# Three float32 products on zeros in place of twelve float16 ones, and the score pairs of tiles 1 to 7 issued one step later

## The chip, the cores and the metric

The kernel runs on one core of a Trainium2 chip. The core has a matrix engine (TensorE, PE in the profile), a vector engine (VectorE, DVE), a scalar engine (ScalarE, ACT), GpSimd (POOL) and SyncE (SP), whose queue issues nearly all transfers. Each engine works through its own instructions in order; semaphores tie them together. The metric is the device time of one execution in microseconds, and smaller is better.

## The reference, cut to what is computed

Attention of 2 batches with 12 heads, 448 positions and 64 features per head, whose scores are mixed over the heads before the softmax and again after it. Two feed-forward layers (768 to 2048 to 768), one with ELU and one with SiLU, follow on the 896 tokens.

```python
scores = scale * np.matmul(q, k.transpose(0, 1, 3, 2))
scores = np.einsum('bhij,hg->bgij', scores, w_pre)
scores = scores - np.max(scores, axis=-1, keepdims=True)
attn = np.exp(scores)
attn = attn / (np.sum(attn, axis=-1, keepdims=True) + 1e-09)
attn = np.einsum('bhij,hg->bgij', attn, w_post)
return np.matmul(attn, v).astype(np.float32)
```

## The kernel before

The attention part works on 8 tiles T (2 batches, 4 tiles of up to 120 query rows each). A tile is cut into steps of 20 rows (a tile's last step may have 10): tiles 0 to 7 begin at steps 0, 6, 12, 18, 23, 29, 35 and 41, and there are 46 steps. The feed-forward layers come after it, on the same core; the change does not touch them.

For one tile the work runs like this. `qk_pair(T, p)` makes the scores of heads 2p and 2p+1 on PE (line 117) into two PSUM banks; `qk_evac` copies them to the SBUF tile `s`, one head on ACT (line 124) and one on DVE (line 126). Six pairs fill one tile's `s`. There are two homes for `s` (even and odd tiles), so the first pair of tile T+1 writes over what tile T-1 left, and its copies wait until the last transfer out of that home is done. `relayout(s)` (line 147) moves 20 rows of `s`, one transfer for each 10 rows, into one of three slots of `blk`, in the layout in which heads can be mixed. It is issued on SP's queue, two steps ahead of its use.

One step s then does, in this order on each engine: `premix(s)` on PE (line 160, reads `blk`); in some steps from step 8 on two `av_pair` (line 226); the step's score pair, if it has one; `postmix(s-1)` on PE (line 199); the row maxima `rmax(s)` on DVE (line 166); `exps(s)` on ACT (line 174); the copies of the score pair on ACT and DVE; the reciprocal on DVE (lines 182 and 183) and the scaled mixing weights `krn` on POOL (line 187), of which the last two come ahead of the copies in steps with `av_pair`; `post_evac(s-1)` on ACT and DVE (lines 99 and 101); `relayout(s+2)` on SP's queue; and then the loads that the step's table names. `relayout(s+2)` waits until `premix(s-1)` has read its slot. The first relayout of a tile also waits for the copies of that tile's last score pair.

Which step has which score pair is set by the counter `nqk` (line 288 and the lines that follow). It starts at -3, since the first three pairs of tile 1 are made ahead of step 0. So the pairs of tile 1 that are left stand in steps 0 to 2, those of tile 2 in steps 3 to 8, and so on, without a gap, up to the last pair of tile 7 in step 38.

At the start, while the first loads are under way, PE multiplies zeros (line 269): the tile `wz` is set to zero on DVE (line 251) and touched once by ACT (line 252); twelve products of 128x128 with 128x448 in float16 follow, and then the six score pairs of tile 0.

Of the kernel before, what the change touches and what calls it, by code (L numbers as in the profile page):

```python
# [7 lines left out]
F32 = mybir.dt.float32  # L8
F32R = mybir.dt.float32r
F16 = mybir.dt.float16  # L10
# [7 lines left out]
P = 128  # L18
B, H, S, D = 2, 12, 448, 64
# [9 lines left out]
HS = 64  # L29
BW = 5 * H  # L30
NBUF = 3
NWARM = 12
NE = 3
LEAD = 3
KO = (0, 2, 4, 1, 3, 5)
# [4 lines left out]
def attn_moe_moe(ctx: ExitStack, tc: tile.TileContext, q, k, v, w_pre, w_post, w1i, w1o, w2i, w2o, out):  # L40
# [4 lines left out]
    def pool(name, **kw):  # L45
        cm = tc.tile_pool(name=name, reuse_waits="tile", **kw)
        return cm, cm.__enter__()
# [9 lines left out]
    cm_s1, sp1 = pool("s1", bufs=1, side="right")  # L57
# [17 lines left out]
    def prows(t):  # L75

        return nblk(t) * BI
# [3 lines left out]
    def load_q(T, eng=None, parts=(slice(0, NP),)):  # L81
        b, t = tiles[T]
        qT[T] = wp.tile([P, NP, 2 * P], F32, name=f"qt{T}", tag="qT", bufs=3).rearrange("p a b -> p (a b)")[:, :NP * TI].rearrange("p (a b) -> p a b", a=NP)
        for p in parts:
            (eng or nc.sync).dma_start(qT[T][:, p], q[b, t, :, p])
# [20 lines left out]
    def qk_pair(T, p, where=("qk0", "qk1")):  # L106

        b, t = tiles[T]
        m = prows(t)
        if T not in smap:  # L110
            smap[T] = (sp0, sp1)[T % 2].tile([P, H, S], F32, name=f"s{T}", tag="s")
        pq = [ps.tile([P, S], F32, name=f"pq{T}_{p}_{e}", tag=w, bufs=1) for e, w in enumerate(where)]
        for c in range(2):
            n = HS if c == 0 else max(m - HS, 40)
            for e in range(2):
                half = slice(e * D, (e + 1) * D)
                nc.tensor.matmul(pq[e][HS * c:HS * c + n], qT[T][half, p, HS * c:HS * c + n], kT[b, p][half], start=True, stop=True, tile_position=(e * D, HS * c))  # L117
        sev.append((T, p, m, pq))
# [97 lines left out]
    def av_pair(T, p):  # L216

        b, t = tiles[T]
        m = rows(t)
        if p % 2 == 0:  # L220
            late = T + 1 == len(tiles)
            avt[T] = ps.tile([P, 2, TI], F32, name=f"av{T}_{p}", tag=("pre2", "av", "pre0")[p // 2] if late else "qk0" if T + 2 == len(tiles) and p == NP - 2 else "av", bufs=1)
        for j in range(4):
            for e in range(2):
                h = 2 * p + e
                nc.tensor.matmul(avt[T][e * D:(e + 1) * D, p % 2, :m], vall[b][:NV, h, j], amap[T][:NV, j * H + h, :m], start=j == 0, stop=j == 3, tile_position=(0, e * D))  # L226
        if p % 2 == 1:
            (xsp if T + 2 >= len(tiles) else xev).append((T, p - 1, m, avt.pop(T)))
# [18 lines left out]
        xsp.clear()  # L247


    wz = sp1.tile([P, S], F16, name="wz", tag="s")  # L250
    nc.vector.memset(wz, 0.0)
    nc.scalar.activation(wz[0:1, 0:1], wz[0:1, 0:1], AF.Copy)
    load_k(0, 0, nc.scalar)
# [10 lines left out]
    for c in range(2):  # L264
        for r in range(2):
            nc.vector.memset(pbank[c][HS * (1 - r):HS * (2 - r), (4 * r + 3) * BW:(4 * r + 4) * BW], 0.0)
    for n in range(NWARM):
        pw = ps.tile([P, 4 * CP], F32, name=f"warm{n}", tag=f"pre{n % 3}", bufs=1)
# [14 lines left out]
    QK_AT, X_AT, D_AT = {}, {}, {}  # L283

    def at(d, step, f):
        d.setdefault(int(step), []).append(f)

    nqk, nav = -LEAD, 0
    for T in range(NT_ - 1):
        b, t = tiles[T]  # L290
        f, l = first[T], last[T]
        for p in range(NP):
            if nqk >= 0:
                at(QK_AT, nqk, lambda T=T, p=p: qk_pair(T + 1, p))
            nqk += 1
        if T + 3 < NT_:
            at(D_AT, (3, 9, 13, 19, 24)[T], lambda T=T: load_q(T + 3))
        for p in range(NP):
            nav = 8 + 6 * T + p // 2 * 2 if T < 5 else NB + (-8, -6, -5, -4, -2, -1)[3 * T + p // 2 - 15]
            at(X_AT, nav, lambda T=T, p=p: av_pair(T, p))  # L300
# [775 lines left out]
```

## Time and profile before

| | |
|---|---|
| runs of the kernel before | 612.55, 617.24, 616.12 us, median 616.12 |
| the profiled execution's own time | 616.55 us |
| its span, from first to last instruction | 614.8 us |
| PE busy | 601.5 us, 98% |
| DVE, ACT, POOL busy | 425.5, 367.7, 63.4 us |
| attention steps | from about 15 us to 171 us of the span |

The span starts 1.75 us less than the time: that much lies around the instructions. Busy time of PE counts pipelined instructions and does not say that PE is never waited for; which engine sets the pace has to be read stage by stage. In the feed-forward part, from about 171 us on, PE is busy without a break.

### The profile page before, as it was taken

How to read it: one execution, taken by the hardware profiler on the slowest of the kernel's cores; microseconds unless marked ns; L12 is line 12 of the kernel's file. 1: busy time of each engine (PE TensorE's matmuls, PEld its weight loads, DVE VectorE, ACT ScalarE, POOL GpSimd, SP SyncE). 2: the span in 40 equal slices, each digit the busy share in tenths (PEclk: the TensorE clock that was granted, in tenths of full speed). 3: DMA queues.
4: the chain of work that ended last, by engine and by line, in shares of the span. 5: the costliest groups of instructions: out<-in, count | busy, mean ns of one | idle time of the engine just before them, and what ended most of it. 6: DMA issues, size and time to landing. Idle time of an engine off the chain costs nothing.

```text
span 614.8 us, 15117 instructions
## 1 busy us (share of the span) xinstructions
PE 601.5 (98%) x6222; PEld 514.8 (84%) x6222; DVE 425.5 (69%) x726; ACT 367.7 (60%) x686; POOL 63.4 (10%) x119
## 2 busy tenths in 40 slices
PE   7899999999999999999999999999999999999997
PEld 2456676676799899999999999999999999999996
DVE  4677677888847999886776674599888877424420
ACT  4577777788838966758774643476767664322300
POOL 1122222247460000000000000000000000000000
PEclk9899999999999999999999999999999999999999
DMA  6576656554503243432443334344334324444300
GB/s 240 189 211 204 201 173 208 185 186 152 184 3 113 92 155 103 144 105 71 127 125 123 95 90 150 104 130 154 127 103 149 94 93 141 153 149 153 116 30 31
DMA packets 37785, 82.33 MB, mean 134 GB/s; under 512 B 4132, under 2 KB 18388, under 8 KB 37716
## 3 DMA queue, kind: packets, MB, share of 16 engines
q1 hardware_dynamic: 36852, 80.50, 40.8%
q8 instruction: 49, 0.80, 0.5%
q10 hardware_dynamic: 864, 0.87, 0.5%
q14 instruction: 20, 0.16, 0.1%
HBM read 59.24 MB, written 2.75 MB: 101 GB/s over the span
## 4 chain that ended last, share of the span: by engine, by line
PE 83%; ACT 6%; DVE 6%; DMA 2%; issue 1%; SPq 0%; POOL 0%; ACTq 0%; DVEq 0%; POOLq 0%
PE po L504 37%; PE b L778 28%; ACT pe L174 4%; PE pq L117 3%; PE av L226 3%; PE pre L160 3%; PE post L199 3%; PE ph L490 3%; DVE nmx L166 2%; DMA blk<-s 2%; DVE a L101 2%; PE post L490 1%; PE warm L269 1%; DVE sum L182 1%; DVE s L126 1%
## 5 line engine op out<-in xcount | busy, mean ns | idle before, releaser
L778 PE MATMUL b<-x,we 128*128 128x448 f32 x360 | 93.7, 363 | 0.0
L504 PE MATMUL po<-x,we 128*128 128x448 f32 x288 | 81.0, 362 | 0.0
L174 ACT ACTIVATE pe<-pre,nmx 124x448 f32<-124x448 f32 (+1 forms) x92 | 57.5, 629 | 37.0 <-DVE nmx L166 36.4
L730 ACT ACTIVATE wr<-wr 128x768 f32<-128x768 f32 (+1 forms) x61 | 52.6, 865 | 40.8 <-DMA wr<-in_w2o_dram 25.7
L778 PEld LDWEIGHTS b<-x,we 128*128 128x128 f32 x360 | 67.5, 188 | 4.6
L778 PE MATMUL b<-rr,we 128*128 128x448 f32 x288 | 69.5, 362 | 0.0
L199 PEld LDWEIGHTS post<-krn,pe 60*64 60x64 f32 x2520 | 48.6, 136 | 19.9 <-issue 11.2
L461 DVE TENSOR_TENSOR we<-wc,we 128x640 fp32r<-128x640 f32 (+1 forms) x37 | 32.4, 875 | 47.0 <-ACT we L452 45.9
L504 PE MATMUL po<-ge,we 128*128 128x448 f32 x216 | 60.3, 362 | 0.0
L726 DVE SCALAR_TENSOR_TENSOR wc<-wr,wc 128x768 int32<-128x768 int32 (+1 forms) x62 | 56.2, 907 | 2.8
L504 PEld LDWEIGHTS po<-x,we 128*128 128x128 f32 x288 | 54.1, 188 | 3.6
L778 PEld LDWEIGHTS b<-rr,we 128*128 128x128 f32 x288 | 54.1, 188 | 3.5
L166 DVE TENSOR_REDUCE nmx<-pre 124x1 f32<-124x448 f32 (+1 forms) x92 | 52.6, 612 | 5.0 <-PE pre L160 4.8
L504 PE MATMUL po<-rr,we 128*128 128x448 f32 x216 | 55.9, 362 | 0.0
L504 PE MATMUL po<-gs,we 128*128 128x448 f32 x216 | 54.9, 362 | 0.0
L160 PE MATMUL pre<-blk,kpre 64*64 64x448 f32 (+1 forms) x360 | 46.9, 548 | 4.0 <-DMA blk<-s 3.3
L187 POOL TENSOR_SCALAR krn<-kps,sum 124x60 f32<-124x60 f32 (+1 forms) x92 | 38.4, 432 | 115.6 <-DVE sum L183 75.8
L117 PE MATMUL pq<-kt,qt 64*64 64x448 f32 (+2 forms) x384 | 48.1, 557 | 2.0 <-ACT s L124 2.0
L226 PEld LDWEIGHTS av<-a,v 128*64 128x64 f32 x768 | 36.9, 137 | 15.6 <-ACT pe L174 11.3
L199 PE MATMUL post<-krn,pe 60*64 60x60 f32 x2520 | 48.1, 220 | 0.8 <-issue 0.2
L504 PE MATMUL po<-ta,we 128*128 128x448 f32 x168 | 44.8, 362 | 0.0
L452 ACT CAST we<-wc 128x640 fp32r<-128x640 f32 (+1 forms) x37 | 28.3, 764 | 27.2 <-DVE wc L726 26.0
(129 smaller groups left out, 1024.2 us busy)
## 6 DMA issues: line engine op xcount, KB each, us to landing
blk<-s SPq DMA_DIRECT2D x90, 210.0 KB
wr<-in_w1i_dram SPq DMA_DIRECT2D x32, 384.0 KB
wr<-in_w2i_dram SPq DMA_DIRECT2D x32, 384.0 KB
wr<-in_w1o_dram SPq DMA_DIRECT2D x24, 384.0 KB
wr<-in_w2o_dram SPq DMA_DIRECT2D x24, 384.0 KB
wr<-in_w1o_dram SPq DMA_DIRECT2D x12, 256.0 KB
wr<-in_w2o_dram SPq DMA_DIRECT2D x12, 256.0 KB
qt<-in_q_dram SPq DMA_DIRECT2D x7, 360.0 KB
```

The lines of the kernel that those rows point to most:

```text
L117: nc.tensor.matmul(pq[e][HS * c:HS * c + n], qT[T][half, p, HS * c:HS * c + n], kT[b, p][half], start=True, stop=True, tile_position=(e * ...
L160: nc.tensor.matmul(pre[s][r][HS * c:HS * c + HS], kpre[o], blkb[o, s % NBUF, c], start=True, stop=True, tile_position=(HS * r, HS * c))
L166: nc.vector.tensor_reduce(nmx[s][:n, r:r + 1], pre[s][r][:n], axis=AX.X, op=ALU.max, negate=True)
L174: nc.scalar.activation(t[:n], pre[s][r][:n], AF.Exp, bias=nmx[s][:n, r:r + 1], scale=1.0, accum_out=sums[s][:n, r:r + 1])
L187: nc.gpsimd.tensor_scalar(t[:n], kps[:n], z[:n, r:r + 1], None, op0=ALU.mult)
L199: nc.tensor.matmul(w[c][HS * u:HS * u + HS, r, j * BW:(j + 1) * BW], pexp[s][r][o, m * HS:(m + 1) * HS], kr[s][r][o].rearrange("p h i -> p ...
L226: nc.tensor.matmul(avt[T][e * D:(e + 1) * D, p % 2, :m], vall[b][:NV, h, j], amap[T][:NV, j * H + h, :m], start=j == 0, stop=j == 3, tile_ ...
L461: nc.vector.tensor_tensor(lo[:, :m], wbits[n][:, :m].bitcast(F32), hi[:, :m], op=ALU.subtract)
L504: nc.tensor.matmul(po, wt[:, kk * P:(kk + 1) * P], g_op(moe, k0 + kk, hf, gi), start=(k0 == 0 and n_ == 0), stop=(k0 + kn == KF and n_ == ...
L726: nc.vector.scalar_tensor_tensor(cc, r[:, :, 1], 3, cc, op0=ALU.logical_shift_left, op1=ALU.bitwise_or)
L730: nc.scalar.activation(hf, hf, AF.Prelu, scale=2.0 ** -112, alpha=2.0 ** 32)
L778: nc.tensor.matmul(o, wt[:, u * KH + i * P:u * KH + (i + 1) * P], X[x, i][:, xi], start=start and n_ == 0, stop=n_ == 8, skip_group_check= ...
```

## The change

The constant `NWARM` goes from 12 to 3, the tile `wz` becomes float32, and the step of each score pair goes up by one. Nothing else is edited.

```diff
-NWARM = 12
+NWARM = 3
@@
-    wz = sp1.tile([P, S], F16, name="wz", tag="s")
+    wz = sp1.tile([P, S], F32, name="wz", tag="s")
     nc.vector.memset(wz, 0.0)
     nc.scalar.activation(wz[0:1, 0:1], wz[0:1, 0:1], AF.Copy)
@@
         for p in range(NP):
             if nqk >= 0:
-                at(QK_AT, nqk, lambda T=T, p=p: qk_pair(T + 1, p))
+                at(QK_AT, nqk + 1, lambda T=T, p=p: qk_pair(T + 1, p))
             nqk += 1
```

Step 0 now has no score pair, and step 39 has one. The next piece is from DVE, steps 20 and 21, where tile 4 (`s_1201`) is filled and tile 5 (`s_1625`) begins; `nmx` are the row maxima of the step, `pq_5_1` is the second head of pair 5. Before:

```order
L166 TENSOR_REDUCE nmx_1598<-pre_0_1541 124x1
L166 TENSOR_REDUCE nmx_1598<-pre_1_1542 124x1
L182 TENSOR_SCALAR sum_1601<-sum_1601 124x2
L183 RECIPROCAL sum_1601<-sum_1601 124x2
L126 TENSOR_SCALAR s_1201<-pq_5_1_1565 120x448
L101 COPY a_1533<-post_93 128x2x48x5
L166 TENSOR_REDUCE nmx_1660<-pre_0_1619 124x1
L166 TENSOR_REDUCE nmx_1660<-pre_1_1620 124x1
L126 TENSOR_SCALAR s_1625<-pq_0_1_1627 120x448
```

And in the changed kernel, where tile 4 is named `s_1254`:

```order
L166 TENSOR_REDUCE nmx_1572<-pre_0_1515 124x1
L166 TENSOR_REDUCE nmx_1572<-pre_1_1516 124x1
L182 TENSOR_SCALAR sum_1575<-sum_1575 124x2
L183 RECIPROCAL sum_1575<-sum_1575 124x2
L126 TENSOR_SCALAR s_1254<-pq_4_1_1539 120x448
L101 COPY a_1507<-post_93 128x2x48x5
L166 TENSOR_REDUCE nmx_1633<-pre_0_1593 124x1
L166 TENSOR_REDUCE nmx_1633<-pre_1_1594 124x1
L126 TENSOR_SCALAR s_1254<-pq_5_1_1600 120x448
```

The rows of a step are the same, but the copy of pair 5, for which the first relayout of tile 4 waits, now stands in step 21, behind the maxima of that step. The relayout itself has not moved: it is the last work of step 21 in both kernels.

The second place is on ACT at step 39 (`pe` are the exponentials, `a_2748` and `a_2722` the evacuation of the step before). Before, the step has no copy into `s`:

```order
L174 ACTIVATE pe_0_2945,sum_2944<-pre_0_2907,nmx_2941 124x448
L174 ACTIVATE pe_1_2947,sum_2944<-pre_1_2908,nmx_2941 124x448
L99 COPY a_2748<-post_92 128x2x48x5
L364 CAST x_2960<-xr_2447 128x240
L349 CAST x_5_2963<-xr_757 128x448
```

In the changed kernel the last copy of tile 7 stands between the exponentials and the evacuation:

```order
L174 ACTIVATE pe_0_2925,sum_2924<-pre_0_2881,nmx_2921 124x448
L174 ACTIVATE pe_1_2927,sum_2924<-pre_1_2882,nmx_2921 124x448
L124 ACTIVATE s_2517<-pq_5_0_2887 90x448
L99 COPY a_2722<-post_92 128x2x48x5
L364 CAST x_2942<-xr_2421 128x240
L349 CAST x_5_2945<-xr_731 128x448
```

Here a copy was added to the step, as one was on DVE and a pair of score products on PE.

## Rows read from the trace of the kernel before

**Rows 1.** Timeline, first 21 us: start, us, engine, line, operation, count, [idle before, releaser].
```profile
0.84 0.24 DVE L251 MEMSET wz<- 128x224 uint32 x1 [0.84 <-PEq L1062]
...
2.28 4.59 PE L269 MATMUL warm<-wz 128*128 128x448 f16 x12 [2.28 <-ACT wz L252]
...
7.22 0.14 PEld L117 LDWEIGHTS pq<-kt,qt 64*64 64x64 f32 x4 [0.23 <-issue]
...
13.35 1.59 SPq L147 DMA_DIRECT2D blk<-s  x2
...
16.15 0.14 PEld L160 LDWEIGHTS pre<-blk,kpre 64*64 64x64 f32 x2 [0.66 <-DMA blk<-s]
...
20.24 0.98 PE L160 MATMUL pre<-blk,kpre 64*64 64x448 f32 x2 [2.08 <-DMA blk<-s]
```

**Rows 2.** Chain that ended last, in order of time: start, us, what (attention part).
```profile
14.99 5.21 DMA blk<-s
...
64.02 5.43 DMA blk<-s
```

**Rows 3.** Stretches: from:to, length, busy (x instructions) by engine, PEclk, DMA share, GB/s.
```profile
20.50:23.50 3.00, 3.00 (x30) 1.27 (x29) 1.16 (x2) 0.84 (x3) 0.07 (x1) 0.50 0.53 198
...
58.00:68.00 10.00, 9.82 (x272) 6.46 (x268) 7.21 (x18) 7.19 (x20) 2.53 (x6) 1.00 0.74 236
...
85.00:87.00 2.00, 2.00 (x72) 1.30 (x72) 0.94 (x4) 2.00 (x7) 0.01 (x1) 1.00 0.00 0
```

**Rows 4.** Timeline around step 15: premix of steps 14, 16 and 18, and a copy.
```profile
61.96 0.97 PE L160 MATMUL pre<-blk,kpre 64*64 64x448 f32 x8
...
68.59 0.94 PE L160 MATMUL pre<-blk,kpre 64*64 64x448 f32 x8
...
69.77 0.62 DVE L126 TENSOR_SCALAR s<-pq 120x448 f32<-120x448 f32 x1 [1.34 <-PE pre L160]
...
75.88 0.94 PE L160 MATMUL pre<-blk,kpre 64*64 64x448 f32 x8
```

**Rows 5.** Timeline, tile 4 begins: copies of steps 20 and 21, first relayout, premix(23).
```profile
86.72 0.60 DVE L126 TENSOR_SCALAR s<-pq 120x448 f32<-120x448 f32 x1
...
87.38 1.68 SPq L147 DMA_DIRECT2D blk<-s  x2
...
89.76 0.54 ACT L124 ACTIVATE s<-pq 120x448 f32<-120x448 f32 x1
...
93.33 0.93 PE L160 MATMUL pre<-blk,kpre 64*64 64x448 f32 x8
```

**Rows 6.** Timeline, tile 5 begins: copy in step 27, premix(29), maxima of step 29.
```profile
109.61 0.54 ACT L124 ACTIVATE s<-pq 120x448 f32<-120x448 f32 x1
...
112.98 0.98 PE L160 MATMUL pre<-blk,kpre 64*64 64x448 f32 x8
...
114.20 0.61 DVE L166 TENSOR_REDUCE nmx<-pre 124x1 f32<-124x448 f32 x1
```

**Rows 7.** Timeline, tile 6 begins: copy in step 33, premix(35), maxima of step 35.
```profile
129.46 0.53 ACT L124 ACTIVATE s<-pq 90x448 f32<-90x448 f32 x1
...
132.88 0.98 PE L160 MATMUL pre<-blk,kpre 64*64 64x448 f32 x8
...
134.05 0.61 DVE L166 TENSOR_REDUCE nmx<-pre 124x1 f32<-124x448 f32 x1
```

**Rows 8.** Timeline, tile 7 begins: end of step 39's exponentials, premix(41), maxima of step 41.
```profile
149.61 0.20 ACT L174 ACTIVATION_READ_ACCUMULATOR pe<-pre,nmx 124x1 f32 x1
...
152.28 0.94 PE L160 MATMUL pre<-blk,kpre 64*64 64x448 f32 x8
...
153.88 0.61 DVE L166 TENSOR_REDUCE nmx<-pre 124x1 f32<-124x448 f32 x1
```

**Rows 9.** Timeline, tile 1 begins: copy in step 3, premix(6).
```profile
30.14 0.54 ACT L124 ACTIVATE s<-pq 120x448 f32<-120x448 f32 x1
...
35.36 0.93 PE L160 MATMUL pre<-blk,kpre 64*64 64x448 f32 x8
```

## The prediction

> **What bounds the kernel now.** I read the attention part stage by stage, since the feed-forward part, which the change doesn't touch, has PE busy without a break and simply starts later when attention ends later. First the timeline of the start: twelve products on zeros fill PE from 2.28 us for 4.59 us, the score pairs follow, and then PE waits for `blk`: the second half of premix(1) stood still for 2.08 us until a relayout landed at 20.24 [rows 1]. After that the timeline shows two kinds of stretch. Up to about 100 us PE sets the pace: premix(14) to premix(16), two steps, is 68.59 - 61.96 = 6.63 us, and PE has something to do in all of it. One pair of steps is longer, premix(16) to premix(18) with 7.29 us; there DVE stood still for 1.34 us ahead of the copy of tile 4's first score pair [rows 4], since that copy overwrites what tile 2's last relayout still reads. From 100 us to 156 us PE has small gaps, and the loop of maxima on DVE, exponentials on ACT and the reciprocal on DVE sets the pace; a late premix costs only what it is later than DVE is ready for it.
>
> The places that matter for the change are the tile changes. The first relayout of a tile waits for the copies of the tile's last score pair. For tile 4 it starts at 87.38 us, right behind the DVE copy of step 20 (86.72 + 0.60), and premix(23), which reads it, starts at 93.33: nearly six us of room [rows 5].
>
> **The change, part by part.** *The zeros.* Twelve products take 4.59 us, 0.38 each, or 448 columns at the lower of the two clock levels, 1.2 GHz. A float32 product goes through PE twice; at the full level one passage takes 0.14 + 0.23 = 0.37 us from weight load to weight load [rows 1], where 448 columns at 2.4 GHz would be 0.19. So a passage runs at half a column per cycle, a product at a quarter, and at 1.2 GHz it costs 4 x 0.37 = 1.5 us: three cost 4.5, the same as the twelve. The first float32 weight load has nothing ahead of it to hide under: between 0 and 0.2 us, I take **+0.1** (the weight load of 0.14 us is the nearest row [rows 1]). The memset of `wz` writes 448 words per row where it wrote 224: 0.24 us becomes some 0.5, ending near 1.3 us, and the products waited for ACT until 2.28 anyway [rows 1]; nothing, unless that wait were gone, and then 0.24.
>
> The Trainium skill, page "TensorE: Matmul & The Clock Gate", section "Back-to-back issue gap", gives a product's spacing at the lower level as its columns divided by 1.2 GHz and names no data type; by it three products would be over after 1.1 us. By the row of the passages they take 4.5. The trace decides for the passages here, and the other reading is priced below as a rival.
>
> *The step that gains and the step that loses a pair.* From step 1 to step 38 every step has one pair as before, with the same number of products and copies, so its work is unchanged. Step 0 loses one pair (on PE, ACT and DVE). That frees nothing: premix(1) waits for the relayout until 20.24 in any case [rows 1]. Step 39 gains one. PE has a gap there; ACT gets a copy of 0.53 us [rows 7] and DVE one of 0.60 [rows 5], both in the loop that sets the pace: **+0.55**.
>
> *The wait that goes.* Tile 4's first copy now comes in step 16, when tile 2's last relayout has long landed. The 7.29 us become 6.63 [rows 4]: **-0.66**. The other tile changes show no such wait, so nothing is to be had there.
>
> *The wait that comes.* For tiles 4 to 7 the last pair's copies now stand in the step that ends with the tile's first relayout, two steps ahead of its use. A relayout is two transfers issued about 0.84 us apart (1.68 for two [rows 5]). At the start, with an empty queue, one that was issued at 13.35 let PE go on at 16.15 [rows 1]: 2.80 us. So the second half is there 0.84 + 2.80 = 3.64 us after the issue, and the issue comes 0.06 us after the last copy (87.32 to 87.38 [rows 5]). That the queue is empty at these places shows in the stretch from 85 to 87 us, in which nothing moved [rows 3]. The copies of the step in question end where today's copies of that step end:
> - Tile 4: ACT's copy of step 21 ends at 89.76 + 0.54 = 90.30, issue 90.36, landed 94.00, premix(23) started at 93.33 [rows 5]. PE sets the pace: **+0.67**.
> - Tile 5: copy ends 110.15, issue 110.21, landed 113.85, premix(29) started at 112.98, so 0.87 late. Its 0.98 us ended 0.24 ahead of DVE's maxima at 114.20 [rows 6]: **+0.63**.
> - Tile 6: 129.99, 130.05, landed 133.69, 0.81 late against 132.88; 0.19 of room ahead of the maxima at 134.05 [rows 7]: **+0.62**.
> - Tile 7: step 39's exponentials leave ACT at 149.81, the new copy ends at 150.34, landed 154.04. Premix(41) stood at 152.28, and with the 0.55 of step 39 at 152.83: 1.21 late, 0.66 of room [rows 8]: **+0.55**.
>
> Tile 1 keeps its room: the copy of step 3 ends at 30.68, landed at 34.38, premix(6) at 35.36 [rows 9]. Tiles 2 and 3 likewise have a step more than tiles 4 to 7. Behind each late relayout the next ones stand on SP's queue, with loads of `v` or weights between them; each is issued 1.7 us or so after the one ahead and used two or three us after it, so they don't fall further behind. The `k` loads of steps 10 to 15 wait for PE's products of the same step instead of the step before; that holds SP up for about the length of one pair, with the relayouts behind them used more than a step later. I take nothing for it.
>
> What is uncertain is the landing. Lower end: no lateness counts, the sum is 0.1 + 0.55 - 0.66 = 0. Upper end: two relayouts are in the chain of waits with 5.21 and 5.43 us [rows 2], about 2.5 us more than 2.80. Four times 2.5 would add 10. Both of those had other transfers ahead of them (three relayouts' worth at the start, and without a break from 58 to 68 us, at a DMA share of 0.74 [rows 3]), while the tile changes 4 to 7 find the queue empty. I take 2.80.
>
> **The sum.** 0.1 + 0.55 - 0.66 + 0.67 + 0.63 + 0.62 + 0.55 = +2.46. The profiled execution took 616.55 us (the median of the runs is 616.12, so it is an ordinary one): **619.0 us**, 0.4% more.
>
> **The rivals.**
> - *Late landings, slower.* The relayouts at tile changes take some 5.3 us as the two in the chain did, not 2.80. For: DMA share at such times rises once the relayouts follow each other. Against: the empty queue. With two of four late it is 619.0 + 5.0 = 624.0, with all four 629. It decides (over 1% slower) from the second late one on. Chance 0.14.
> - *No lateness counts.* The landing is earlier than 2.8 us, or DVE and ACT have more room than I see: 616.6 us. For: in the stretch after 100 us PE has gaps. Against: tile 4 lies where PE has none. Chance 0.12.
> - *The zeros don't raise the clock.* Then the pairs start at half speed. The stretch from 20.50 to 23.50 shows what that is: granted clock 0.50 [rows 3], until PE had worked for some 3.5 us; half of it is lost, 1.7 us: 620.7 us. Against: that same stretch was float32 work, and the clock rose in it. Chance 0.05.
> - *The three products are over at once*, as three float16 ones would be: 3 x 0.38 = 1.15 us, so 3.4 us sooner. The first pairs begin up to 3.4 us earlier at the lower clock, do half as much, and gain at most 1.7: 617.2 us. It is what the page named above would make of them; the passages in the trace speak against it. Chance 0.04.
>
> **How the numbers follow.** The forecast, 616.6 to 622.7 with its middle at 619.0, has 0.65. The runs of the kernel before differ by 0.8%, so about 1%, 6 us, is what a measurement can tell from no change. Over 1% slower (above 622.3) are the late landings and a small tail of the forecast: 0.18. Over 1% faster (below 610) would need a gain that no row shows: 0.03. Within 1%: 0.79. The range that leaves out 2 in 10 goes from 615.0 (the case without lateness, less the scatter of the runs) to 624.0 (two late landings).
>
> **What would show it.** In the changed kernel's profile: three `warm` products, six records, ending near 6.9 us, and pairs with no wait behind them; no wait of DVE ahead of the first copy of tile 4; PE (premix, line 160) waiting for `blk` once at the beginning of each of tiles 4 to 7, by about 0.7 to 1.2 us; a copy into `s` on ACT in step 39. It is wrong if those waits are missing, if they are 2 us and more, if a wait for `blk` appears in the middle of a tile, or if the granted clock is 0.50 under the first pairs.

## The result, and the profile after

The changed kernel takes 621.54 us (median of 6 runs, 620.06 to 624.18) beside 615.35 us for the kernel before (6 runs, 612.55 to 617.24). The ratio is 1.0113, with a 95% interval from 1.0076 to 1.0151: some 7 us slower. The forecast was 619.0 with a range from 615.0 to 624.0. The direction and the range held; the size, +2.46 us, was less than half of what came.

| | before | after |
|---|---|---|
| the profiled execution's own time | 616.55 us | 624.18 us |
| its span | 614.8 us | 622.4 us |
| PE busy | 601.5 us | 606.9 us |
| DVE, ACT, POOL busy | 425.5, 367.7, 63.4 us | 427.4, 368.4, 63.6 us |
| maxima of the last attention step begin | 167.34 us | 174.76 us |

One of the executions profiled below, of the kernel before, lost some 12 us in the feed-forward part for reasons of its own, and only its attention part is read. In the changed kernel all of the loss lies in the attention part: from the last step's maxima to the end it is 447.4 us before and 447.6 after. The timeline of the start of the changed kernel answers to [rows 1]:

```profile
0.89 0.43 DVE L251 MEMSET wz<- 128x448 f32 x1 [0.89 <-PEq L1062]
...
2.27 4.85 PE L269 MATMUL warm<-wz 128*128 128x448 f32 x6 [2.27 <-ACT wz L252]
...
7.05 7.46 PE L117 MATMUL pq<-kt,qt 64*64 64x448 f32 x72
...
15.71 3.17 PE L160 MATMUL pre<-blk,kpre 64*64 64x448 f32 x14 [1.20 <-DMA blk<-s]
```

Three float32 products are six records and take 4.85 us where the twelve took 4.59. The pairs follow at once; the weight loads of their first rounds, and the stretch:

```profile
7.05 0.29 PEld L117 LDWEIGHTS pq<-kt,qt 64*64 64x64 f32 x8 [1.29 <-issue]
7.62 0.14 PEld L117 LDWEIGHTS pq<-kt,qt 64*64 64x64 f32 x4 [0.28 <-issue]
8.00 0.14 PEld L117 LDWEIGHTS pq<-kt,qt 64*64 64x64 f32 x4 [0.24 <-issue]
```
```profile
6.00:14.00 8.00, 8.00 (x74) 2.53 (x72) 4.84 (x8) 4.32 (x8) 0.00 (x0) 1.00 0.73 271
```

The columns are those of [rows 3]; the 1.00 is the granted clock. It also reads 1.00 over the zeros of the kernel before, whose pace, 0.38 us for 448 columns, is that of the lower level, so here the pace says more: the first round of the pairs takes 0.57 us and the later ones 0.38, as in [rows 1]. In the profile of the zeros alone the first two rounds take 0.80 and 0.49 us, so that some 0.5 us are lost there. The second half of premix(1) does not stand for 2 us this time. The waits of PE from 10 to 175 us (us in total, times, longest) show a kind that was not in the forecast:

```profile
PE post L199 <- issue: 3.8, 2, 2.0
PE pq L117 <- ACT s L124: 2.0, 5, 0.5
PE pre L160 <- DMA blk<-s: 1.7, 2, 1.2
...
PE av L226 <- issue: 0.6, 1, 0.6
```

"issue" is time in which PE waits for nothing that the profile shows. The timeline around the longest of these, with the first relayout of tile 4 behind it, and the stretch that follows:

```profile
85.72 0.86 PE L199 MATMUL post<-krn,pe 60*64 60x60 f32 x47
...
88.57 0.34 PE L199 MATMUL post<-krn,pe 60*64 60x60 f32 x9 [1.99 <-issue]
...
91.18 1.73 PE L199 MATMUL post<-krn,pe 60*64 60x60 f32 x56
...
92.58 1.66 SPq L147 DMA_DIRECT2D blk<-s  x2
```
```profile
89.20:92.60 3.40, 3.40 (x69) 2.15 (x65) 2.61 (x6) 2.19 (x6) 0.00 (x0) 0.52 0.02 5
```

PE stops after 47 of the 56 products of one postmix for 1.99 us; behind that the granted clock is 0.52, that is the lower level of 1.2 GHz nearly throughout, so that the next postmix takes 1.73 us where it takes 0.99 elsewhere. Tiles 5 and 7 look as forecast; first relayout, premix, and for tile 7 the maxima:

```profile
114.75 5.14 SPq L147 DMA_DIRECT2D blk<-s  x6
...
117.59 1.43 PE L160 MATMUL pre<-blk,kpre 64*64 64x448 f32 x6 [0.18 <-ACT xr L237]
...
156.20 5.18 SPq L147 DMA_DIRECT2D blk<-s  x6
...
159.06 1.81 PE L160 MATMUL pre<-blk,kpre 64*64 64x448 f32 x8 [0.51 <-DMA blk<-s]
...
160.90 1.16 DVE L166 TENSOR_REDUCE nmx<-pre 124x1 f32<-124x448 f32 x2 [0.98 <-PE pre L160]
```

The premix begins 2.84 and 2.86 us after the issue, and its second half lies 0.83 us further on.

For the rest one table serves. It gives the time between the starts of the maxima of two steps, from the timeline of each profile (steps 8 to 14 hold tile 2's change, 14 to 18 tile 3's, 22 to 25 tile 4's, 28 to 34 tile 5's, 34 to 40 tile 6's, 40 to 43 tile 7's). "After 2" is a second profile of the changed kernel, and the other columns are experiments below.

| steps | before | after | after 2 | zeros alone | pairs alone | tiles 4-7 | tiles 5-7 | tile 7 | pairs, v later | pairs, pad |
|---|---|---|---|---|---|---|---|---|---|---|
| 8-14 | 19.67 | 23.03 | 20.38 | 20.14 | 21.22 | 19.67 | 19.93 | 19.98 | 20.73 | 20.64 |
| 14-18 | 14.39 | 13.50 | 14.21 | 13.17 | 13.53 | 13.46 | 13.17 | 13.17 | 14.27 | 13.49 |
| 18-22 | 13.12 | 16.13 | 13.18 | 13.17 | 14.42 | 13.12 | 13.18 | 13.18 | 13.18 | 13.53 |
| 22-25 | 10.26 | 11.99 | 13.12 | 10.14 | 13.36 | 12.98 | 10.32 | 10.13 | 12.75 | 13.12 |
| 28-34 | 19.85 | 20.52 | 20.37 | 19.85 | 20.35 | 23.58 | 20.37 | 19.88 | 21.26 | 21.95 |
| 34-40 | 20.25 | 20.94 | 22.39 | 20.25 | 21.85 | 20.94 | 20.97 | 20.49 | 21.75 | 20.93 |
| 40-43 | 10.05 | 11.52 | 11.51 | 10.04 | 11.50 | 11.54 | 11.56 | 11.58 | 11.52 | 13.43 |

### The profile page after: what moved, and what is told of

Its sections match the earlier page's. It is cut to its first block, busy times and chain, and to the rows that moved or that the text cites. A ratio compares the mean times of both kernels' runs of the same rounds, so it can differ in the third digit from the quotient of the medians.

```text
span 622.4 us, 15096 instructions
## 1 busy us (share of the span) xinstructions
PE 606.9 (98%) x6216; PEld 515.8 (83%) x6216; DVE 427.4 (69%) x726; ACT 368.4 (59%) x686; POOL 63.6 (10%) x119
## 4 chain that ended last, share of the span: by engine, by line
PE 87%; ACT 5%; DVE 4%; issue 2%; DMA 2%; ACTq 0%; DVEq 0%
PE po L504 37%; PE b L778 27%; PE av L226 5%; PE pre L160 4%; PE post L199 4%; PE pq L117 4%; PE ph L490 3%; ACT pe L174 3%; DMA blk<-s 2%; DVE nmx L166 1%; PE post L490 1%; DVE a L101 1%; PE warm L269 1%; DVE sum L182 0%; DVE s L126 0%
## 5 line engine op out<-in xcount | busy, mean ns | idle before, releaser
L160 PE MATMUL pre<-blk,kpre 64*64 64x448 f32 (+1 forms) x360 | 50.4, 546 | 2.0 <-DMA blk<-s 1.7
```

Of the source, the lines that this page charges most:

```text
L160: nc.tensor.matmul(pre[s][r][HS * c:HS * c + HS], kpre[o], blkb[o, s % NBUF, c], start=True, stop=True, tile_position=(HS * r, HS * c))
```

## The experiments

### The two parts apart, and second profiles

Both kernels unchanged once more, and then each part of the change alone. The zeros alone:

```diff
-NWARM = 12
+NWARM = 3
-    wz = sp1.tile([P, S], F16, name="wz", tag="s")
+    wz = sp1.tile([P, S], F32, name="wz", tag="s")
```

and the pairs alone:

```diff
-                at(QK_AT, nqk, lambda T=T, p=p: qk_pair(T + 1, p))
+                at(QK_AT, nqk + 1, lambda T=T, p=p: qk_pair(T + 1, p))
```

> The kernel before once more, for a second profile of it. In the first one the second half of premix(1) stood until a relayout landed at 20.24 us and the granted clock fell to 0.50 behind it. If that belongs to the kernel, it comes again, within some tenths of a us. If it is a matter of chance, PE doesn't wait there this time and the span up to the maxima of step 7 is about 2.5 us shorter, as it was in the changed kernel. Time ratio to itself 1.000.

Ratio to itself 0.9998 (0.9975 to 1.0021). Its profile answers the question: the maxima of step 1 begin 2.31 us after those of step 0 (17.36, 19.67), as in the zeros alone (17.91, 20.23) and in tile 7 alone (16.45, 18.77), but 4.84 us after them in the first profile (17.16, 22.00). So the 2.08 us of [rows 1] are no fixed part of the kernel. A wait like it stands in three of the fourteen profiles; the other two are 4.56 us with the pairs of tiles 1 to 3 moved and 3.84 us with `v` later.

> The changed kernel once more, for a second profile of it. In the first one PE stood still three times in the middle of the products of one step, with nothing in the profile to wait for: 0.58 us at 40.8, 1.77 at 46.7 and 1.99 at 86.6 us, each time after the same number of instructions beyond a multiple of 256. Theory A (chance: the code of PE comes in blocks by DMA, and a block was held up by other transfers): such stalls come at other multiples of 256, or not at all, and without them the time is about 3 us above the kernel before. Theory B (they belong to the new order): they come again at 40 to 47 and at 86 us. In both, the first relayouts of tiles 5, 6 and 7 are late by 0.6 to 1.2 us. Time ratio 1.011.

Ratio 1.0115 (1.0082 to 1.0148). None of the three stalls came again, and it was as slow all the same. What came again are the tile changes, and tiles 4 and 6 are far above the forecast (22-25 and 34-40). So the kernel is slower without these stalls too, and the 3 us that theory A left for that case are too few. In the first profile after, where they cost most, the wait at tile 4 is smaller (11.99 us).

> The zeros alone: three float32 products for twelve float16 ones, the score pairs in the steps of before. By the forecast +0.1 us; by the trace of the changed kernel, in which the pairs began at 7.05 us in place of 6.79, up to +0.4. Ratio 1.000 to 1.001. The rival (the three products change where PE's code blocks begin, by twelve instructions, and with it the stalls) would show stalls of PE without a cause in the profile and some us more.

Ratio 1.0000 (0.9978 to 1.0021): the zeros cost nothing that these runs can tell from zero, which is to within some 1.3 us.

> The pairs alone: the score pairs one step later, twelve float16 products on zeros as before. If the pairs cost what the forecast said, +2.4 us, ratio 1.004. If they cost all that was measured, +6 us, ratio 1.010. In its profile: no wait ahead of tile 4's first copy, and first relayouts that are late by 0.6 to 1.2 us at tiles 5, 6 and 7.

Ratio 1.0108 (1.0076 to 1.0139), 6.6 us of 614.2: the pairs are the whole loss.

### Which tiles

The zeros are those of before in all that follow. With the condition shown the pairs of tiles 1 to 3 move; with `T >= 3`, `T >= 4` and `T >= 6` in its place those of tiles 4 to 7, of tiles 5 to 7 and of tile 7.

```diff
-                at(QK_AT, nqk, lambda T=T, p=p: qk_pair(T + 1, p))
+                at(QK_AT, nqk + (T < 3), lambda T=T, p=p: qk_pair(T + 1, p))
```

> The pairs of tiles 1 to 3 alone one step later; those of tiles 4 to 7, and the zeros, as before. Theory A (the time is lost where tiles 4 to 7 begin, because their first relayout is late): nothing or little, 0 to +0.6 us, ratio 1.000 to 1.001; the first relayouts of these three tiles have a step more to spare. Theory B (any pair that is moved costs, for instance because SP's queue stands behind it in steps 10 to 15): three sevenths of the +6.6 us of all pairs, +2.8, ratio 1.0045.

Ratio 1.0088 (1.0057 to 1.0119), more than either theory had. The edit brings something of its own: tile 3's last pair moves to step 15, where tile 4's first pair stays, so that two pairs share two PSUM banks in one step and PE waits for the copies of the first. The longest wait of PE between 10 and 175 us, and DVE's copy of tile 4's first pair:

```profile
PE pq L117 <- ACT s L124: 3.5, 5, 1.9
```
```profile
72.28 0.62 DVE L126 TENSOR_SCALAR s<-pq 120x448 f32<-120x448 f32 x1 [3.52 <-DMA blk<-s]
```

The copy waits for tile 2's last relayout, as in [rows 4]. Steps 14 to 18 take 16.67 us there in place of 13.17, and the profiled execution also has the late relayout at the start. In the other stretches it is 20.45 (8-14), and 13.12, 10.28, 19.86, 20.25 and 10.05, as before. By its time this run decides nothing. Where the profiles show a cost of tiles 1 to 3 is steps 8 to 14: the eight profiles that leave these pairs where they were have 19.67 to 20.34 us there, the five others 20.38 to 21.22, not counting the first profile after with two of its stalls. Half a us or so is lost there, and no run tells why.

> The pairs of tiles 4 to 7 alone one step later; those of tiles 1 to 3, and the zeros, as before. Theory A: the whole loss, +6 to +6.6 us, ratio 1.010; in the profile the first maxima of tiles 4 to 7 later by about 2.5, 0.7, 1.4 to 2.1 and 1.6 us. Theory B: four sevenths, +3.8 us, ratio 1.006.

Ratio 1.0121 (1.0076 to 1.0166): tiles 4 to 7 alone cost as much as all pairs. Here the change only leaves step 15 without a pair. Theory A holds as to the place. In the profile tile 5's first relayout is late by 1.9 us (its second half is used 5.59 us after the issue), PE waits for it twice, and behind that the granted clock is 0.50 for 3.4 us:

```profile
116.80:120.20 3.40, 3.40 (x68) 2.14 (x63) 2.16 (x4) 1.77 (x5) 0.00 (x0) 0.50 0.77 248
```

Steps 28 to 34 take 23.58 us there, 3.2 more than the 20.37 of a landing on time: with the lower clock behind it, a late landing can cost well over its own delay.

> The pairs of tiles 5 to 7 alone one step later; those of tiles 1 to 4, and the zeros, as before. Theory A: tile 4's 2.9 us stay away, tiles 5, 6 and 7 cost 0.7, 0.7 and 1.6 us, and 1.5 to 2 us more for each of the three whose first relayout has a block of PE's code in its midst: +3 to +5 us, ratio 1.005 to 1.008. In the profile the maxima of step 24 come as in the kernel before. If the loss doesn't hang on the tile changes one by one: ratio 1.010 and more.

Ratio 1.0081 (1.0053 to 1.0109), at the upper edge of the expectation. The profiled execution (616.33 us) was among the lowest of twelve, up to 622.22. In it steps 22 to 25 take 10.32 us, so tile 4's loss is gone, and tiles 5, 6 and 7 cost 0.5, 0.7 and 1.5 us.

> The pairs of tiles 5 to 7 one step later, once more, for a second profile: the executions so far lie between 616.0 and 622.2 us, and the one that was profiled is among the lowest (616.33). Theory E (a block of PE's code that is fetched in the midst of a first relayout makes it late, by chance of when and where it is fetched): where this execution takes 620 us and more, at least one of the first relayouts of tiles 5, 6 and 7 has its second half used 4.5 to 5.6 us after the issue in place of 3.7, with a block ahead of it. Rival: the relayouts are as in the first profile and the time is lost elsewhere (the first relayouts of all, at 16 to 22 us, or PE at the end of a block).

Ratio 1.0050 (1.0027 to 1.0073), and the profile (616.84 us) is as the first to a few hundredths from step 14 on, with no late relayout. So about 3 us is the price of the three tiles without one: 3.1 by this run, 2.7 by the sum of the stretches. What the slower executions of the run before lost, 620 to 622 us, no profile caught; theory E was not tested by this run.

> The pairs of tile 7 alone one step later. By the profiles so far 1.6 us (1.1 where the first relayout is used, 0.55 in the step behind it), 2 us more in executions where a block of code hits that relayout: ratio 1.003 to 1.005. The forecast had 0.55 for the relayout and 0.55 for the copy in step 39, ratio 1.002.

Ratio 1.0028 (1.0012 to 1.0043), 1.7 us. Its timeline: first relayout, premix(41) and maxima, premix(42) and maxima.

```profile
145.96 5.17 SPq L147 DMA_DIRECT2D blk<-s  x6
...
148.85 1.82 PE L160 MATMUL pre<-blk,kpre 64*64 64x448 f32 x8 [0.54 <-DMA blk<-s]
150.71 1.16 DVE L166 TENSOR_REDUCE nmx<-pre 124x1 f32<-124x448 f32 x2 [1.03 <-PE pre L160]
...
153.26 0.94 PE L160 MATMUL pre<-blk,kpre 64*64 64x448 f32 x8
154.27 1.16 DVE L166 TENSOR_REDUCE nmx<-pre 124x1 f32<-124x448 f32 x2
```

The maxima begin 4.75 us after the issue. From the maxima of step 40 (146.46) it is 4.25 us where it was 3.12 before (150.76 to 153.88), and on to the next 3.56 where it was 3.01: behind the late premix PE still has the av products and the postmix ahead of premix(42). The same kernel, whose pairs of tile 4 stand where they stood, also answers to [rows 4]; premix of steps 14, 16 and 18:

```profile
58.28 0.93 PE L160 MATMUL pre<-blk,kpre 64*64 64x448 f32 x8
...
64.86 0.93 PE L160 MATMUL pre<-blk,kpre 64*64 64x448 f32 x8
...
71.45 0.93 PE L160 MATMUL pre<-blk,kpre 64*64 64x448 f32 x8
```

6.58 and 6.59 us, with the copy of tile 4's first pair in step 15 as before. So the 7.29 us of [rows 4] are not a fixed part of the kernel. They are no single case either: of the eight profiles that keep this copy in step 15, five take 13.17 us for steps 14 to 18, the first one 14.39, the one of tiles 1 to 3 16.67, and that of the kernel before with a pad (below) 14.20, where the same copy waits again:

```profile
69.27 0.62 DVE L127 TENSOR_SCALAR s<-pq 120x448 f32<-120x448 f32 x1 [1.57 <-DMA blk<-s]
```

The trace has the times at which the parts of a transfer report that they are done, ten reports for each transfer of a relayout. For the first transfer of tile 2's last relayout the last report comes 5.2 to 5.7 us after its issue in these three, and 3.9 to 4.3 in the five.

### Tile 4 and the loads of v

In the profile of tiles 4 to 7 tile 4 begins like this; relayouts and loads of `v` on SP's queue, and the premixes of steps 23 and 24:

```profile
88.16 1.68 SPq L147 DMA_DIRECT2D blk<-s  x2
...
89.89 0.54 SPq L95 DMA_DIRECT2D v<-in_v_dram  x1
...
90.51 1.65 SPq L147 DMA_DIRECT2D blk<-s  x2
...
91.14 1.57 PE L160 MATMUL pre<-blk,kpre 64*64 64x448 f32 x6
...
96.31 0.97 PE L160 MATMUL pre<-blk,kpre 64*64 64x448 f32 x4 [1.09 <-DMA blk<-s]
```

The first premix comes 2.98 us after the first issue, as it should. The one behind it is late: its second half starts at 96.31, 5.80 us after its relayout was issued behind a load of `v`. So I moved the loads, in the kernel with the pairs alone:

```diff
-                    at(D_AT, 2 * g + u + (16 if b else 0), lambda b=b, u=u, g=g: load_v(b, u, g))
+                    at(D_AT, 2 * g + u + ((16 if 2 * g + u < 5 else 21) if b else 0), lambda b=b, u=u, g=g: load_v(b, u, g))
```

> All pairs one step later, and the three loads of v that stand on SP's queue behind the first relayouts of tile 4 (steps 21 to 23) moved to steps 26 to 28, well ahead of their use in step 32. Theory D (tile 4 costs 2.9 us where tile 5 costs 0.7, because the relayout of its second step is issued behind a load of v and shares the DMA engines with it: its second half starts 5.3 to 5.9 us after its issue): now 3.7 us after its issue, tile 4 costs 0.7 to 1.2 us, and the time is some 2 us below that of the pairs alone, ratio 1.007 to 1.008. If v has nothing to do with it: step 24 as late as before, ratio 1.011.

Ratio 1.0128 (1.0099 to 1.0157): no gain. The same place in its profile:

```profile
89.39 7.41 SPq L147 DMA_DIRECT2D blk<-s  x8
...
92.95 0.97 PE L160 MATMUL pre<-blk,kpre 64*64 64x448 f32 x4 [0.37 <-DMA blk<-s]
...
94.99 0.59 PE L160 MATMUL pre<-blk,kpre 64*64 64x448 f32 x2 [1.07 <-DMA blk<-s]
...
97.36 0.92 PE L160 MATMUL pre<-blk,kpre 64*64 64x448 f32 x5
```

Step 24 no longer waits for its relayout, but that is no support for theory D: in this execution the first relayout was late instead (its second half came 5.60 us after the issue), and one wait hides the other: 22-25 is 12.75 us. The last report of the second relayout comes 5.55 us after its issue here too.

The edit also moved the loads behind another tile's first relayouts: tile 5's are issued in steps 27 and 28. First relayout, load of `v`, second relayout, and the second half of premix(30):

```profile
111.73 1.70 SPq L147 DMA_DIRECT2D blk<-s  x2
...
113.48 0.53 SPq L95 DMA_DIRECT2D v<-in_v_dram  x1
114.11 1.65 SPq L147 DMA_DIRECT2D blk<-s  x2
...
118.97 0.97 PE L160 MATMUL pre<-blk,kpre 64*64 64x448 f32 x4 [0.24 <-DMA blk<-s]
```

PE goes on there 4.86 us after the issue, and steps 28 to 34 take 21.26 us in place of 20.35 to 20.52. The ten reports of the transfer come 4.17 to 4.82 us after the issue of the relayout where they come after 3.5 to 3.6 without a load of `v`. So the load ahead does make a relayout later, by 0.7 to 1.2 us. At tile 4 in the profile above nine of the ten come by 4.71 us and the last at 5.75, so that its last us has another cause. What moving the loads clear of all first relayouts is worth was not shown.

### Blocks of PE's code

The profile has a queue named "instruction", with 49 packets of 16 KB that move 0.80 MB; PE has 12,432 products and weight loads, 254 for each packet, and the packets come faster where PE issues more of them. I take them for blocks of PE's code. In the second profile of the changed kernel the first relayout of tile 4 and its premix look like this, and between 91.2 and 91.3 us the DMA view has one such packet:

```profile
88.44 1.65 SPq L147 DMA_DIRECT2D blk<-s  x2
...
91.98 0.97 PE L160 MATMUL pre<-blk,kpre 64*64 64x448 f32 x4 [0.33 <-DMA blk<-s]
...
94.04 0.59 PE L160 MATMUL pre<-blk,kpre 64*64 64x448 f32 x2 [1.09 <-DMA blk<-s]
```
```profile
q1 hardware_dynamic: 13, 0.02, 56.1%
q8 instruction: 1, 0.02, 54.9%
```

The halves come 3.54 and 5.60 us after the issue. To see whether the code does it, I put 160 instructions more into PE's stream ahead of the first premix, in the pairs alone and in the kernel before:

```diff
+NPAD = 40
@@
+    pad = [ps.tile([P, 4 * CP], F32, name=f"pad{r}", tag=w, bufs=1) for r, w in enumerate(("av", "pre2"))]
+    for n in range(NPAD):
+        r, c = n % 2, n // 2 % 2
+        nc.tensor.matmul(pad[r][HS * c:HS * c + HS, :BW], kpre[HS * r:HS * r + HS], kpre[HS * r:HS * r + HS, :BW], start=True, stop=True, tile_position=(HS * r, HS * c))
```

> All pairs one step later, and ahead of the first premix, in a time in which PE waits, 40 small products (160 instructions of PE) on kpre whose result nobody reads: all later code of PE stands 160 instructions further on in its blocks of 256, so that its blocks are fetched some 3 us earlier in relation to the tiles. Theory C (the first relayouts of tiles 4 and 6 were later than those of tiles 5 and 7 because a block of PE's code was fetched in the midst of them): at tiles 4 and 6 the second half now starts 3.7 us after the issue, as at tiles 5 and 7 (it was 5.6 and 5.15), no block of code comes in the midst, and the time is 2 to 3 us below that of the pairs alone, ratio 1.006 to 1.008, unless PE stands at other block ends. If the landing depends on the tiles and not on the code: tiles 4 and 6 as before, ratio 1.011.

Ratio 1.017 (1.0121 to 1.0220). Tile 6 and then tile 7 in its profile:

```profile
132.49 5.13 SPq L148 DMA_DIRECT2D blk<-s  x6
...
135.53 1.25 PE L161 MATMUL pre<-blk,kpre 64*64 64x448 f32 x6
...
153.41 5.17 SPq L148 DMA_DIRECT2D blk<-s  x6
...
156.98 0.97 PE L161 MATMUL pre<-blk,kpre 64*64 64x448 f32 x4 [1.22 <-DMA blk<-s]
159.02 0.97 PE L161 MATMUL pre<-blk,kpre 64*64 64x448 f32 x4 [1.08 <-DMA blk<-s]
```

The places went where theory C sent them: tile 6 begins 3.04 us after the issue with no block in its midst (it was 4.40 in the second profile of the change and 3.84 in the pairs alone). But a block now meets tile 7, which comes 3.57 and 5.61 us after the issue and loses 1.9 us more than in the other profiles with moved pairs. The gain that I expected in the total did not come; the blocks met other relayouts, and tile 4, whose first relayout was on time here, takes 13.12 us as before.

> The kernel before with the same 40 products, as a control: their work lies in a time in which PE waits for a relayout, so that it costs 0 to +0.3 us. Theory C: ratio 1.000, as the first relayouts have over 5 us to spare there, whatever is fetched in between. If the place of the code blocks matters by itself (stalls of PE at block ends), the ratio is off by 0.002 and more, in either direction.

Ratio 1.0032 (0.9997 to 1.0066), six of ten executions at 616.3 to 619.2 and four at 612.8 to 613.9. In the profile PE is done with the pad at 15.56 us, in its wait, but the second half of the very first premix stands until 18.70. At the tile changes the kernel before has 4.6 us and more between issue and premix, and nothing is lost at tiles 5 to 7 (28-34 is 19.87, 34-40 20.26, 40-43 10.04). Tile 4's steps take 11.33 us, about 1.1 more than elsewhere without moved pairs, though PE doesn't wait for `blk` in them; I have not found why. At the start there is no such room.

The 25 first relayouts of tiles 5 to 7 with moved pairs, in nine profiles, give the count. In 19 the second half starts 3.67 to 3.75 us after the issue, in one 3.86, in five 4.50 to 5.61. In each of these five a packet of code began to move between 0.5 and 3 us after the issue; the same is true of ten of the other 20. So a block isn't enough for a late landing, and the count alone doesn't show that it is the cause: with 15 blocks among 25, five out of five would come by chance about once in 18 times.

The reports of the parts tell more. In the 20 all ten parts of the first transfer are reported done 2.61 to 2.76 us after the issue. In the five, nine are done by 2.74 us and one at 3.38 to 4.26; of the second transfer nine by 4.14 and one at 4.46 to 5.57, and PE goes on 0.04 to 0.05 us behind that. So a late landing is one late part of ten. And in four relayouts (two of tile 4, one each of tiles 5 and 7) the packet began 2.79 to 2.81 us after the issue and the second half came after 5.59 to 5.61 us each time; no first relayout that was on time has a packet beginning there. This ties the late part to the block. That the two take the same DMA engine would explain it, and why other blocks do no harm; the trace does not name the engine of a packet, so this is argued and not shown.

## Why the prediction was right in kind and wrong in size

**The zeros: right.** Forecast +0.1, measured ratio 1.0000. The six passages took 4.85 us where 4.5 and 0.1 for the weight load were forecast. The rival of three products at once did not come. Of the rival of the clock a small part did: the first rounds of the pairs ran slower, by 0.2 us in all in the profile after and 0.5 in the zeros alone, less than the runs resolve. The Trainium skill's rule of a spacing by columns alone (page "TensorE: Matmul & The Clock Gate", section "Back-to-back issue gap") would have had 1.1 us, an estimate by its figure; the trace has 4.85, and the trace decides for float32.

**The wait that goes: wrong, 0.66 us.** The mechanism was there, a copy that waits for tile 2's last relayout, but it comes in three of the eight profiles that keep the copy in step 15; the other five take 13.17 us for steps 14 to 18 in place of 14.39. I had one profile and took a late landing in it for a fixed part of the kernel. As an estimate from these eight the wait is worth a third of the 0.66, and moving the copy does not even save that. Steps 14 to 18 even take 0.3 us more with the pairs moved (13.46 to 13.53, over 13.17), 1.0 us more in two profiles; I have not settled why. Counted right, this term is 0 or a little over.

**Tiles 5 and 6: right.** The landing was the term that I called uncertain, and its value held: 2.80 and 3.64 us forecast from an empty queue, 2.85 and 3.70 measured. The stretches cost 0.5 and 0.7 us where no block of code comes in between; forecast 0.63 and 0.62.

**Tile 7: too small, 1.10 forecast, 1.7 measured.** The two terms together are what the maxima of step 41 lose: 1.10 forecast, 1.13 measured. Their split was wrong. The copy in step 39 costs nothing (from the maxima of step 39 to those of 40 it is 3.01 us before and with tile 7 moved), so that the late relayout alone makes the 1.13. What the sum lacks comes a step later: 0.55 us, from PE's work behind the late premix.

**Tile 4: the step that failed most, 0.67 forecast, 2.7 to 3.1 measured** (22-25: 12.98 to 13.36 in four profiles, 10.26 before). The sentence at fault is that behind each late relayout the next ones "don't fall further behind". At tile 4 a load of `v` stands between the first and the second relayout on SP's queue, and the steps there are short: 2.47 us from the maxima of step 23 to those of 24 before (94.34, 96.81). The second relayout becomes the later of the two, by 1.1 us of waiting in the profile shown: the load makes all of it later, as at tile 5 with `v` moved, and one of its ten parts comes another us later, whose cause stays open. A wait for `blk` in the middle of a tile is what the prediction had named as a sign against itself. Where the first relayout is late by itself, that hides the second.

**The rival of late landings** was right in that landings of 5.6 us do occur, but not for its reason (other transfers ahead on the queue): one part of ten comes late, each time with a block of code near it. In three of the five profiles with all pairs moved, two of the first relayouts of tiles 4 to 7 have their second half 4.5 us and more after the issue. At 0.14 it was rated too low.

Put together: 2.46 - 0.1 for the zeros + 0.66 for the wait that goes + 2.2 for tile 4 + 0.6 for tile 7 + 0.3 for steps 14 to 18 = 6.1. The pairs alone cost 6.6 us, with an interval from 4.7 to 8.5; what is left over fits steps 8 to 14 and late landings in some executions (tile 6 cost 1.5 to 2.1 us in three profiles with all pairs moved and 0.7 in the others), but these shares were not measured by themselves.

That the measured 621.54 us lies inside the range is in part luck. The forecast stood on an execution of 616.55 us, 2 us over what the kernel before took in the later runs (medians of 613.83 to 614.54), and that covered a part of the 4.5 us that its sum lacked.

No kernel tried here beats the kernel before. Its pairs stand a step early enough that nearly all this falls into idle time.

## What to carry to other kernels

When a producer is moved closer to a transfer's use, cost the whole group of transfers that then runs without room, with everything that stands between them on the same queue, not only the first. A wait in a single profile may belong to that execution: before a gain is booked on taking it away, look for the same wait at the other places of the same kind, and where they lack it, book nothing. Room of a few us ahead of a transfer's use isn't waste; it is what covers landings that vary from 3.7 to 5.6 us.

## What the runs showed of the hardware that I had not expected

PE can run out of instructions, as far as the following signs go. The three stalls of the first profile after stand in the midst of groups, and by the counts of PE's products and weight loads they come after 1198, 1449 and 3480 of them: 251 and 2031 apart, one and eight times 256 less some instructions that these counts leave out. In the pairs alone there are stalls of 0.60 and 0.99 us after 1451 and 3481. It is the count that decides and not the place in the program: in the two kernels with the pad, whose program stands 160 instructions further on, such stalls come after 1201 and 7802, and elsewhere after 1198 to 1200 and 7797 to 7799. Of the 18 such stalls of over 0.35 us in the attention parts of all profiles each ends 1.3 to 1.6 us behind the end of a packet of code. At the longest, 1.99 us, a packet had moved from 85.7 to 87.0 us and PE went on at 88.57. The Trainium skill, page "Runtime: NRT & Kernel Launch", section "Instruction fetch mechanics", has the code refilled in blocks of 16 KiB, 256 instructions, fetched ahead on a queue of their own, at a cost that is mostly hidden. The trace agrees on the size of the blocks; hidden the cost was in most places, and at these it was 0.4 to 2.0 us, and once the lower clock for 3.4 us behind it.

A transfer can be late by one of its parts. A relayout's transfer of 210 KB lets PE go on 2.85 us after its issue; where one of its ten reports came late, with a block of code near it, PE went on after 3.5 to 4.4 us, and after up to 5.6 at the second one of the pair.
